# Hedgehog attention into a ReGLU feed-forward: first keys turned in fp32 on TensorE, a new head of the order

## The chip, the cores and the metric

One core of one Trainium2 chip runs the whole program. The metric is device time in microseconds of one execution; of several executions the median counts. A profiled execution also has a span, from its first to its last instruction, which is a little shorter than its time. The engines are named as in the profile: PE (TensorE), DVE (VectorE), ACT (ScalarE), POOL (GpSimd), SP (SyncE, which here only issues transfers).

## The reference

Eight batches, eight heads, 576 tokens of 64 numbers, all in float32. `phi` projects a token by the 64x128 matrix `w_phi`, takes the largest absolute value away and keeps both exponentials. The output of the attention, one row of 512 numbers a token, goes through a feed-forward with a ReLU gate (512 to 1536 and back).

```python
def phi(x):
    proj = np.einsum('bhsd,df->bhsf', x, w_phi)
    proj = proj - np.max(np.abs(proj), axis=-1, keepdims=True)
    return np.concatenate([np.exp(proj), np.exp(-proj)], axis=-1)
kv = np.einsum('bhsf,bhsd->bhfd', k_p, v)
num = np.einsum('bhsf,bhfd->bhsd', q_p, kv)
den = np.einsum('bhsf,bhf->bhs', q_p, z)[..., None] + 1e-06
gate = np.maximum(x @ w_gate, 0.0)
return (gate * (x @ w_val) @ w_out)
```

## The kernel before

All engines are programmed by one list of words, `ORDER`. Each word is a step (`do_..`), its arguments, after a colon the PSUM banks it uses, after an at sign the slot of a ring of buffers that it takes. There is no scheduler: on every engine the instructions stand in the order of the words, and an engine that waits holds up all that stands behind it on that engine. Waits between engines come from the tiles that the steps read and write.

A batch b is worked on in 512 tokens (a token row p holds tokens 4p to 4p+3, called i = 0 to 3) and 64 left over, which go two batches at a time into a ninth, mixed tile. The eight heads are cut in three groups j: heads 0 and 1, 2 to 4, 5 to 7. The mixed tokens of the keys ride with group 0, as its third "head".

- Loads. `lf` (SP, line 445) brings keys of heads 2 to 4 of batch 0 as fp32 into a tile that is free at that time, `cf` and `cg` (DVE and ACT, line 453) cast them to bf16. `lk`, `lq`, `lm` load the other keys, the queries and the mixed keys through POOL, which casts them on the way (lines 434, 466, 473); `lv` and `lw` load v and its mixed tokens (496, 520); `wl` and `wo` load thirds of the three large weights through POOL (528, 534). `wr` loads `w_phi` from ACT's queue (393), `wd` casts it on DVE (402), `w1` and `wa` make a second arrangement of it on PE and ACT.
- Keys of batch 0. `k0` turns six blocks of 128x128 on PE (584), `k1` copies them to kT on DVE (587), `k2` projects a group with twelve matmuls into four banks, one for each i (605). `ke` on ACT takes the two exponentials of each bank into kp (614), `kx` on DVE its largest absolute values into mk (622). `kk` (ACT, 631) makes from mk the two factors ek by which v is scaled; `kp` (ACT, 642) writes the same factors into 24 spare columns of a bank, from where DVE can read them.
- v. `vs` scales a group of v on POOL by ek (669), `vd` does it on DVE with the factors in the bank (651), `vo` and `vp` fill the last column on POOL and DVE (681, 659), `vq` scales the mixed v (line 697, POOL). Before, in batch 0, groups 0 and 1 and the mixed v are POOL's, group 2 DVE's. `kv` is the product of kp and the scaled v on PE (718), copied by ACT (`kc`, 729).
- Queries. `q0`, `q1`, `qb` turn and project them (746, 754, 764; from batch 1 on `qt`, `qc`, 769 and 778), `qe` takes the exponentials on ACT (793), `qx` the largest absolute values on DVE into maxq (801), `qy` turns maxq on PE (811), `qz`, `qu`, `qw` make of it the factor cq for one i.
- Attention's output. `nu` multiplies by kv (841), `nt` and `nv` join the halves on DVE (862, 872), `nr` takes the reciprocal (880), `nx` scales on POOL into xu (884). In batch 0 `xp` on PE and `xa` on ACT turn xu into xT (906, 920); later batches go by a transposing transfer, `xt`.
- Feed-forward. `pv` and `pg` (1029) are the value and gate products of one i in batch 0, four blocks of f at a time, `fv` and `fg` (1000) those of a whole group of 512 tokens. `pa`, `va` copy to val on ACT, `pb`, `ga` multiply on DVE (1050, 1021); `fo` is the product with w_out (1061), `fp` the last ones in halves (1092).
- `zz.n` is n matmuls of zeros, 128x256, into a bank that nobody reads (425). They have no place in the result; they stand in the first 28 us.

Of the kernel before, what the change touches and what calls it, by code (L numbers as in the profile page):

```python
# [16 lines left out]
ms.0 ms.4@vr0 wr ms.3@vr1 lf id sl ms.5 ms.6 ms.2 lw.0.1 lw.0.0 if cf.1 lk.0.2 lk.0.0 wd cg.0  # L17
zz.18:0 k0.1:0 k1.1:0@kT0 lm.0.1 lm.0.0 zz.1:1 w1:2 lq.0.1 lq.0.0 wa:2 zz.2:1 k2.1:0345
ke.0.1.2.0:4@kp0 lv.0.2 kx.0.1.1:3@mk0 lv.0.1 ke.0.1.3.1:5 kx.0.1.2:4 zz.2:1 k0.2:2 k1.2:2@kT1
ke.0.1.1.0:3 ke.0.1.2.1:4 kx.0.1.0:0 kx.0.1.3:5 ke.0.1.1.1:3 zz.7:1 k2.2:2674 ke.0.2.0.1:2@kp1  # L20
ke.0.2.2.0:7 kx.0.2.1:6@mk1 ke.0.2.0.0:2 ke.0.1.0.0:0 k0.0:3 k1.0:3@kT1 wl.0.0 ke.0.1.3.0:5
kx.0.2.2:7 kx.0.2.0:2 lv.0.0 zz.6:1 q0.1:3 q1.1:3@qT0 ke.0.2.1.1:6 ke.0.2.2.1:7 kx.0.2.3:4 zz.1:1
q0.0:5 q1.0:5@qT1 ke.0.2.1.0:6 zz.4:1 k2.0:2736 lm.1.1 lk.1.3 lm.1.0 kx.0.0.0:2@mk2 ke.0.1.0.1:0
kx.0.0.2:3 ke.0.2.3.0:4 kx.0.0.1:7 kp.0.2.1:4 kk.0.1.0@ek0 lq.1.2 kk.0.1.1 qb.1.0:0 qe.0.1.0.1:0@qp0
vo.1@vs0 kp.0.2.0:4 kx.0.0.3:6 vp.2:4@vs1 vs.0.1.0 qb.1.1:5 qe.0.1.1.0:5@qp1 qe.0.1.0.0:0 qx.0.1.1:5
ke.0.0.1.0:7@kp2 qx.0.1.0:0 vd.0.2.0:4 vs.0.1.1 kk.0.0.0@ek1 ke.0.0.3.0:6 zz.18:1 qb.0.1:0
ke.0.0.2.1:3 ke.0.0.1.1:7 qx.0.0.1:0 qb.0.2:7 qx.0.0.2:7 ke.0.2.3.1:4 wl.0.1 kk.0.0.1 vq.0.1
ke.0.0.0.1:2 ke.0.0.3.1:6 ke.0.0.0.0:2 zz.6:1 qb.0.0:6 vs.0.0.0@vs2 vq.0.0 qx.0.0.0:6 zz.5:1
# [1124 lines left out]
```

## Time and profile before

| what | value |
|---|---|
| three timed runs | 376.44, 376.68, 373.83 us; median 376.44 |
| the profiled execution's own time | 377.31 us |
| its span | 375.5 us |
| PE busy, share of the span | 367.3 us, 98% |
| DVE busy | 290.4 us, 77% |
| ACT busy | 228.5 us, 61% |
| POOL busy | 157.3 us, 42% |
| mean granted TensorE clock | 0.990 |

The profiled execution takes 1.8 us more than its span and is 0.87 us above the median of the runs. A timeline row holds start, duration, engine, line, operation, output and input, and a count where neighbours were merged; in square brackets stands how long the engine was idle before it and what ended that. The view by windows gives for each stretch its length and then, for each engine, busy time and number of instructions, the granted clock, the share of the DMA engines and what they moved.

### The profile page before, as it was taken

Reading aid. Unit: us, or ns where it says so; the run is one execution under the profiler, and the core shown is the slowest. Engines: PE = TensorE matmul, PEld = TensorE weight load, DVE = VectorE, ACT = ScalarE, POOL = GpSimd, SP = SyncE. Lnnn points to the kernel's source line nnn. Section 1 sums busy time; section 2 is a strip of 40 time slices with the busy share of each in tenths; the row PEclk is TensorE's granted clock in tenths of the full one; section 3 lists DMA queues with packets and bytes.
Section 4 is the critical chain, followed back from the end, with each engine's and each line's share of the span. In section 5 each row is a group of like instructions: output and inputs, shape, how many; then the busy total and the mean of one; then the engine's idle time right before and its main releaser. Section 6 shows DMA issues by size and latency. Waiting matters only on the chain.

```text
span 375.5 us, 9202 instructions
## 1 busy us (share of the span) xinstructions
PE 367.3 (98%) x3614; PEld 196.7 (52%) x3614; DVE 290.4 (77%) x672; ACT 228.5 (61%) x550; POOL 157.3 (42%) x163
## 2 busy tenths in 40 slices
PE   8798999999999999999999999999999999999996
PEld 5567857446544554564455444554444644444444
DVE  5969999998989899999978795888675646534441
ACT  4979996999768873987865556846764301212111
POOL 8774496549349138912770343513045013100000
PEclk9969999999999999999999999999999999999999
DMA  9999998973974992393438052183330022200114
GB/s 141 248 201 199 149 133 119 151 117 58 176 184 71 181 139 70 68 190 76 100 61 152 17 95 66 46 148 51 107 89 17 2 72 82 58 2 15 41 30 141
DMA packets 90381, 38.10 MB, mean 101 GB/s; under 512 B 64226, under 2 KB 85602, under 8 KB 90338
## 3 DMA queue, kind: packets, MB, share of 16 engines
q0 software_dynamic: 33504, 15.03, 31.4%
q1 hardware_dynamic: 56560, 22.29, 26.7%
q8 instruction: 28, 0.46, 0.5%
q10 hardware_dynamic: 274, 0.20, 0.2%
q14 instruction: 15, 0.12, 0.1%
HBM read 37.81 MB, written 9.44 MB: 126 GB/s over the span
## 4 chain that ended last, share of the span: by engine, by line
PE 93%; DVE 2%; DMA 2%; POOL 1%; ACT 1%; issue 0%; POOLq 0%; ACTq 0%
PE bank L1000 47%; PE bank L1061 24%; PE bank L718 6%; PE bank L841 4%; PE bank L1029 4%; PE bank L778 2%; PE bank L562 2%; DMA qn<-in_q_dram 2%; PE bank L982 1%; PE bank L1092 1%; PE bank L764 0%; PE bank L425 0%; POOL kn L434 0%; DVE mk L622 0%; DVE u L872 0%
## 5 line engine op out<-in xcount | busy, mean ns | idle before, releaser
L1061 PE MATMUL bank<-wo,h 128*128 128x512 bf16 x420 | 97.8, 379 | 0.0
L614 ACT ACTIVATE kp<-bank 128x384 bf16<-128x384 f32 x192 | 83.5, 509 | 16.4 <-PE bank L562 11.2
L1015 ACT CAST val<-bank 128x512 bf16<-128x512 f32 x81 | 47.2, 594 | 73.1 <-PE bank L1000 67.5
L1021 DVE SCALAR_TENSOR_TENSOR h<-bank,val 128x512 bf16<-128x512 f32 x100 | 67.1, 681 | 28.9 <-PE bank L1000 14.4
L1000 PE MATMUL bank<-xTs,wv 128*128 128x512 bf16 x352 | 87.1, 379 | 0.0
L1000 PE MATMUL bank<-xTs,wg 128*128 128x512 bf16 x352 | 86.4, 379 | 0.0
L884 POOL TENSOR_TENSOR xu<-u,r 128x512 bf16<-128x512 f32 x36 | 37.2, 1040 | 99.2 <-DVE r L880 72.5
L793 ACT ACTIVATE qp<-bank 128x512 bf16<-128x512 f32 x128 | 70.0, 619 | 10.7 <-PE bank L778 9.0
L1061 PEld LDWEIGHTS <-h 128*128 128x128 bf16 x420 | 39.2, 98 | 45.8 <-issue 2.4
L669 POOL TENSOR_TENSOR vs<-vn,ek 128x780 bf16<-128x780 f32 (+3 forms) x40 | 52.8, 1341 | 24.0 <-ACT ek L631 13.4
L1000 PEld LDWEIGHTS <-wg 128*128 128x128 bf16 x400 | 37.5, 98 | 41.6 <-issue 1.1
L1000 PEld LDWEIGHTS <-wv 128*128 128x128 bf16 x400 | 37.0, 98 | 41.1 <-issue 1.3
L622 DVE TENSOR_REDUCE mk<-bank 128x3 f32<-128x384 f32 x96 | 49.7, 541 | 3.5 <-ACT kp L614 1.4
L801 DVE TRANSPOSE_TENSOR_REDUCE maxq<-bank 128x16 f32<-128x512 f32 x64 | 42.4, 693 | 7.1 <-ACT qp L793 3.2
L872 DVE TENSOR_TENSOR u<-bank,t 128x195 f32<-128x195 f32 (+1 forms) x108 | 33.8, 331 | 2.4 <-POOL xu L884 0.4
L862 DVE TENSOR_TENSOR t<-bank,cq 128x195 f32<-128x195 f32 (+1 forms) x96 | 29.9, 327 | 7.0 <-PE bank L841 6.2
L841 PEld LDWEIGHTS <-qp 128*128 128x128 bf16 x512 | 22.5, 98 | 11.9 <-issue 1.5
L697 POOL TENSOR_TENSOR vr<-vm,ek 64x520 bf16<-64x520 f32 x16 | 16.9, 1055 | 23.4 <-ACT ek L631 15.9
L841 PE MATMUL bank<-kv,qp 128*128 128x65 bf16 x512 | 25.3, 193 | 0.0
L718 PEld LDWEIGHTS <-kp 128*128 128x128 bf16 x640 | 23.0, 101 | 3.9 <-ACT qp L793 1.0
L718 PE MATMUL bank<-vs,kp 128*128 128x65 bf16 x512 | 23.8, 198 | 0.0
L1070 ACT COPY ob<-bank 128x512 f32<-128x512 f32 x19 | 11.3, 595 | 20.4 <-PE bank L1061 19.5
(97 smaller groups left out, 355.2 us busy)
## 6 DMA issues: line engine op xcount, KB each, us to landing
out_dram<-ob SPq DMA_DIRECT2D x31, 256.0 KB, 2.4
vn<-in_v_dram SPq DMA_DIRECT2D x24, 256.0 KB, 4.2
kn<-in_k_dram POOLq DMA_DIRECT2D x7, 512.0 KB, 9.7
qn<-in_q_dram POOLq DMA_DIRECT2D x7, 512.0 KB, 7.6
wv<-in_moe_w_val_dram POOLq DMA_DIRECT2D x3, 512.0 KB, 11.4
wg<-in_moe_w_gate_dram POOLq DMA_DIRECT2D x3, 512.0 KB, 8.6
wo<-in_moe_w_out_dram POOLq DMA_DIRECT2D x3, 512.0 KB, 7.7
out_dram<-ob SPq DMA_DIRECT2D x9, 128.0 KB, 2.3
```

Of the source, the lines that this page charges most:

```text
L614: nc.scalar.activation(kp_of(3 * b + j)[:, i, s].rearrange("p n f -> p (n f)"), bank[bk[0]][:, 0 : 3 * F], AF.Exp, scale=(1.0, -1.0)[s],)
L622: nc.vector.tensor_reduce(mk_of(3 * b + j)[:, :, i], bank[bk[0]][:, 0 : 3 * F].rearrange("p (n f) -> p n f", f=F), axis=AX.X, op=ALU.max, ...
L669: nc.gpsimd.tensor_tensor(vs_of(3 * b + j)[:, s, 0:n].rearrange("p n i e -> p (n i) e")[:, :, 0:e], src[:, lo:hi].rearrange("p h i e -> p ...
L718: nc.tensor.matmul(out_ps[:, h - lo, s, :], lhsT=lhsT, rhs=rhs, start=(at == 0), stop=(at == 2 * n * (C + 1) - 1),)
L793: nc.scalar.activation(qp_of(4 * b + i)[:, s, 4 * hq : 4 * hq + 4].rearrange("p h m -> p (h m)"), bank[bk[0]], AF.Exp, scale=(1.0, -1.0)[s],)
L801: nc.vector.tensor_reduce(maxq[:, :, i, 4 * hq : 4 * hq + 4].rearrange("p t h -> p h t"), bank[bk[0]].rearrange("p (h t u) -> p h t u", h= ...
L841: nc.tensor.matmul(bank[bk[0]][:, E * n : E * (n + 1)], lhsT=qp_of(4 * b + i)[:, s, h, :], rhs=kv_of(b)[:, h, s, 0:E],)
L884: eng.tensor_tensor(xu_of(n).rearrange("p (h d) -> p h d", d=D), u_of(n)[:, :, 0:D], r_of(n).to_broadcast([P, H, D]), op=ALU.mult,)
L1000: nc.tensor.matmul(bank[bk[0]], lhsT=w[:, dc, P * f : P * f + P], rhs=xT(g)[:, dc, :], start=(dc == 0), stop=(dc == NDC - 1),)
L1015: nc.scalar.copy(val_of(NFC * g + f), bank[bk[0]])
L1021: nc.vector.scalar_tensor_tensor(h2_of(g, f), bank[bk[0]], 0.0, val_of(NFC * g + f), op0=ALU.max, op1=ALU.mult)
L1061: nc.tensor.matmul(bank[bk[0]], lhsT=h2_of(g, f)[:, P * t : P * t + P], rhs=wo_sb[:, f, :], start=(f == 0), stop=(f == NFC - 1),)
```

## The change

The words of `ORDER` are all new from the first one on, but not the work: apart from the start of batch 0, before and after hold the same steps. From `qc.2.1` on, which starts at 81.7 us in the profile of before, PE's 418 steps are the same in the same sequence. What differs by step:

- `kf`, `kh`, `kg`, `k3` for the first group (heads 2 to 4) in place of `cf`, `cg`, `k0.1`, `k1.1`, `k2.1`: PE turns the fp32 keys as they came, six blocks of 128x128 fp32 in two banks, ACT copies the one half (pairs i = 0, 1) and DVE the other to kT as bf16, and `k3` projects half a group (two values of i) with six matmuls into two banks. The other groups are projected by `k3` halves too, in place of `k2`.
- `wq` in place of `wr`: `w_phi` is loaded from SP's queue, behind `lf`.
- Batch 0's v: DVE now scales group 0 (`vd`, eight blocks of 64 in place of twelve) and the mixed v (`vz`, new, two instructions), with factors from bank 2; POOL scales group 2 in place of group 0 and the mixed v.
- Batch 0's query maxima go to four separate tables, one for each i (`maxq0`, in a part of h2 that is not yet used), so that `qy` for one i reads only that table. It is set to zero by `ms.9`.
- `zz`: 76 zero matmuls instead of 75, 20 times instead of 12, in smaller groups.
- Rings: mk and ek have 6 buffers, vs 4, qp 5 (before 3, 3, 3, 4). `nh` and `ni` are defined and not used.

```diff
-    mk_of = ring("mk", 3, [P, 3, 4], FP32)
-    ek_of = ring("ek", 3, [P, 2, 3, 4], FP32)
-    vs_of = ring("vs", 3, [P, 2, 3, 4, EP], BF16)
+    mk_of = ring("mk", 6, [P, 3, 4], FP32)
+    ek_of = ring("ek", 6, [P, 2, 3, 4], FP32)
+    vs_of = ring("vs", 4, [P, 2, 3, 4, EP], BF16)
...
-ms.0 ms.4@vr0 wr ms.3@vr1 lf id sl ms.5 ms.6 ms.2 lw.0.1 lw.0.0 if cf.1 lk.0.2 lk.0.0 wd cg.0
+ms.0 lf ms.2 lm.0.0 ms.4@vr0 ms.6 id lk.0.2 lk.0.0 wq ms.3@vr1 if ms.5 zz.12:7 kf.0:0 ms.9 kf.1:1 wd
...
+    def do_kf(bk, cp):
+        for n in range(3):
+            nc.tensor.matmul(
+                bank[bk[0]][:, P * n : P * n + P],
+                lhsT=k_first()[:, n, P * cp : P * cp + P],
+                rhs=identf,
+                is_transpose=True,
+            )
...
+    def do_k3(bk, j, cp):
+        T = kT_of(j).rearrange("p n m a -> p (n m a)").rearrange("p (k m) -> p k m", m=P)
+        heads = [1, 2, 0] if j == 0 else [0, 1, 2]
+        for k_, n in enumerate(heads):
+            for e in range(2):
+                r = slice(D * e, D * (e + 1))
+                nc.tensor.matmul(
+                    bank[bk[e]][:, F * n : F * (n + 1)],
+                    lhsT=T[r, 2 * k_ + cp, :],
+                    rhs=w64[r, :],
+                    start=(k_ == 0),
+                    stop=(k_ == 2),
+                )
+
+    def do_vz(bk, hh):
+        r = slice(SM * hh, SM * (hh + 1))
+        nc.vector.tensor_tensor(
+            vr_of(0)[r, :, :, hh, 0:E],
+            vm_of(0)[r][:, None, :, :].to_broadcast([SM, 2, 4, E]),
+            bank[bk[0]][r, 3 * F : 3 * F + 24]
+            .rearrange("p (s n i) -> p s n i", s=2, n=3)[:, :, 0, :, None]
+            .to_broadcast([SM, 2, 4, E]),
+            op=ALU.mult,
+        )
...
     def do_qx(bk, b, hq, i):
         nc.vector.tensor_reduce(
-            maxq[:, :, i, 4 * hq : 4 * hq + 4].rearrange("p t h -> p h t"),
+            (maxq0[:, i] if b == 0 else maxq)[:, :, i, 4 * hq : 4 * hq + 4].rearrange("p t h -> p h t"),
```

On DVE, from the cast of the first keys on, the order of before is this (kn are the keys in bf16, w64 is `w_phi`, mk the maxima of a group, qT the turned queries):

```order
L453 COPY kn_0_71<-xTm_144 128x256
L402 COPY w64_148<-w64f_146 128x128
L587 COPY kT_0_77<-bank0_63 128x768
L622 TENSOR_REDUCE mk_0_85<-bank3_66 128x3
L622 TENSOR_REDUCE mk_0_85<-bank4_67 128x3
L587 COPY kT_1_78<-bank2_65 128x768
```

and in the changed kernel, at the same place:

```order
L404 COPY w64_156<-w64f_154 128x128
L376 COPY sel_158<-ident_157 64x256
L627 COPY kT_0_77<-bank1_64 128x3x128
L669 TENSOR_REDUCE mk_0_85<-bank3_66 128x3
L669 TENSOR_REDUCE mk_0_85<-bank2_65 128x3
L669 TENSOR_REDUCE mk_0_85<-bank5_68 128x3
L590 COPY kT_1_78<-bank0_63 128x768
```

The cast is gone, the copy to kT is half as long and stands behind the cast of `w_phi`, and three of the four maxima of the first group now stand ahead of the second group's copy.

On POOL, from the start of batch 0's scaled v on, before (vs is the scaled v, vr the scaled mixed v, xu the attention's output, wv and wg the weights of the value and gate products, qm mixed queries):

```order
L681 COPY vs_0_91<-ek_0_88 128x24
L669 TENSOR_TENSOR vs_0_91<-vn_0_75,ek_0_88 128x12x64 x2
L528 DMA wv_141<-in_moe_w_val_dram 128x4x512
L697 TENSOR_TENSOR vr_1_95<-vm_0_76,ek_1_89 64x8x65
...
L681 COPY vs_2_93<-ek_1_89 128x2x8
L528 DMA wg_140<-in_moe_w_gate_dram 128x4x512 x2
L528 DMA wv_141<-in_moe_w_val_dram 128x4x512
L484 DMA qm_0_74<-in_q_dram 64x8x64
L884 TENSOR_TENSOR xu_0_124<-u_0_118,r_0_121 128x512
```

and after:

```order
L730 COPY vs_2_99<-ek_1_92 128x24
L718 TENSOR_TENSOR vs_2_99<-vn_0_75,ek_1_92 128x12x64 x2
L481 DMA km_0_72<-in_k_dram 128x1x128
L531 DMA wg_148<-in_moe_w_gate_dram 128x4x512
...
L933 TENSOR_TENSOR xu_2_134<-u_2_128,r_2_131 128x512
L481 DMA km_0_72<-in_k_dram 128x1x128
L933 TENSOR_TENSOR xu_3_135<-u_0_126,r_0_129 128x512
L531 DMA wv_149<-in_moe_w_val_dram 128x4x512
L730 COPY vs_3_100<-ek_2_93 128x24
L531 DMA wg_148<-in_moe_w_gate_dram 128x4x512
```

The scaled mixed v is gone from POOL; the last third of wv, which was issued ahead of the first xu, now stands behind all four of them, and the last third of wg behind a copy of batch 1's factors.

513 lines of the change are left out of this document (268 added, 245 removed).

## Prediction

> **What bounds the kernel now.** I read the page first, then the view by windows, cut where the clock or the kind of work changes, then the timeline of the first 46 us. The page:
>
> ```profile
> PE 367.3 (98%) x3614; PEld 196.7 (52%) x3614; DVE 290.4 (77%) x672; ACT 228.5 (61%) x550; POOL 157.3 (42%) x163
> PEclk9969999999999999999999999999999999999999
> PE 93%; DVE 2%; DMA 2%; POOL 1%; ACT 1%; issue 0%; POOLq 0%; ACTq 0%
> ```
>
> The span is PE's: 93% of the chain that ended last is matmuls. One slice, the third, has a clock of 0.6. The windows tell where time can be won (length, then busy time and count of PE, PEld, DVE, ACT, POOL; granted clock, DMA, GB/s):
>
> ```profile
> 7.00:16.40 9.40, 7.94 (x96) 5.67 (x93) 9.02 (x19) 8.97 (x26) 7.55 (x10) 1.00 1.26 243
> 16.40:19.80 3.40, 2.03 (x12) 0.97 (x12) 2.72 (x5) 2.77 (x10) 2.65 (x4) 1.00 1.47 188
> 19.80:23.20 3.40, 3.39 (x16) 1.02 (x15) 2.91 (x5) 3.40 (x8) 3.40 (x5) 0.51 1.37 202
> 23.20:26.70 3.50, 3.50 (x62) 3.44 (x60) 1.96 (x5) 1.41 (x4) 2.57 (x4) 0.50 1.17 207
> 26.70:32.10 5.40, 4.30 (x102) 3.48 (x101) 5.04 (x23) 5.19 (x15) 1.07 (x2) 1.00 1.22 197
> 32.10:37.50 5.40, 5.38 (x97) 4.67 (x97) 5.27 (x18) 5.30 (x13) 2.80 (x3) 1.00 1.30 198
> 37.50:46.10 8.60, 8.60 (x167) 7.82 (x165) 8.60 (x17) 7.78 (x20) 3.91 (x5) 1.00 1.14 161
> 46.10:81.70 35.60, 35.58 (x458) 20.27 (x458) 34.55 (x86) 31.53 (x83) 21.93 (x24) 1.00 1.08 138
> 81.70:375.50 293.80, 290.63 (x2590) 145.39 (x2589) 217.07 (x491) 159.85 (x378) 105.17 (x97) 1.00 0.44 83
> ```
>
> From 32.1 us on PE has no hole but the last 3 us, where the last rows leave; behind 81.7 its order is untouched. So the change can only move the point at which PE becomes full, and whether DVE, busy 34.55 of 35.60 us up to 81.7, lets PE stay full. Three things are seen ahead of 32.1: DVE and ACT are nearly full from 7 us on, PE waits for them between 16.4 and 19.8 (2.03 of 3.40), and after that PE runs 6.9 us at half clock, just when batch 0's kv is made.
>
> **First keys.** The rows of today, from the landing of the fp32 keys to the first exponential:
>
> ```profile
> 1.06 4.02 PE L425 MATMUL bank<-zero 128*128 128x256 bf16 x18 [1.06 <-DVE zero L412]
> 4.05 0.43 DVE L453 CAST kn<-xTm 128x256 bf16<-128x256 f32 x1 [0.91 <-DMA xTm<-in_k_dram]
> 4.87 0.85 PE L584 MATMUL bank<-ident,kn 128*128 128x128 bf16 x6
> 5.64 0.28 DVE L402 CAST w<-w64f 128x128 bf16<-128x128 f32 x1 [1.16 <-DMA w64f<-in_w_phi_dram]
> 5.79 0.55 DVE L587 COPY kT<-bank 128x768 bf16<-128x768 bf16 x1
> 6.59 0.51 PE L605 MATMUL bank<-w,kT 64*128 64x128 bf16 x12
> 7.13 6.08 ACT L614 ACTIVATE kp<-bank 128x384 bf16<-128x384 f32 x15 [0.39 <-PE bank L605]
> 7.40 0.34 PEld L584 LDWEIGHTS <-kn 128*128 128x128 bf16 x6 [0.26 <-DMA kn<-in_k_dram]
> 26.18 0.64 PE L811 MATMUL bank<-identf,maxq 128*128 128x128 f32 x2
> 26.41 0.49 ACT L729 CAST kv<-bank 128x390 bf16<-128x390 f32 x1 [0.67 <-PE bank L718]
> ```
>
> Keys land at 4.05 and the first exponential starts at 7.13. In the changed kernel the cast is gone. Twelve zeros end near 1.06 + 12 x 0.22 = 3.7, so PE stands free. An fp32 transpose is shown by L811: two take 0.64 at half clock, so three take about 0.85: 4.95. ACT's copy of half a group is nearest to L729, 0.49: 5.5. Six projections in place of twelve, half of 0.51 plus the pipe: 6.0. The first exponential starts at 6.05, 1.1 us earlier; DVE's half copy ends near 6.2, and its first maximum stands 0.8 us earlier than today. fp32 transposes are bounded by 0.6 (full clock) and 1.3 (twice the row), which moves this by 0.25 less or 0.45 more.
>
> This needs `w_phi` by 5.5. Today its cast waits until 5.64 and would end at 5.92; if the new queue brings nothing, the first exponential comes at 6.5, 0.6 us earlier than today and not 1.1. On SP's queue it is issued second, ahead of both loads of mixed v that now fill the queue, so I take the early end. [...] POOL's first transfer is now the half of the mixed keys, so the keys of the next group are issued one such issue later; I let PE have them at 7.5, where it takes them off the transfer at 7.40 today.
>
> **From there to the first kv.** Rows for the prices on DVE, and for what PE waits for:
>
> ```profile
> 12.12 0.62 PE L746 MATMUL bank<-ident,qn 128*128 128x128 bf16 x8 [0.57 <-DMA qn<-in_q_dram]
> 13.60 1.95 DVE L622 TENSOR_REDUCE mk<-bank 128x3 f32<-128x384 f32 x4
> 16.78 0.92 DVE L651 TENSOR_TENSOR vs<-vn,bank 128x768 bf16<-128x768 f32 x1
> 17.62 1.30 DVE L801 TRANSPOSE_TENSOR_REDUCE maxq<-bank 128x16 f32<-128x512 f32 x2
> 18.53 1.05 POOL L697 TENSOR_TENSOR vr<-vm,ek 64x520 bf16<-64x520 f32 x1 [0.67 <-issue]
> 22.89 0.40 PE L718 MATMUL bank<-vs,kp 128*128 128x65 bf16 x4
> 23.16 0.41 PE L718 MATMUL bank<-vs,kp 128*128 128x65 bf16 x4
> 26.82 0.29 PE L718 MATMUL bank<-vs,kp 128*128 128x65 bf16 x4
> 26.97 0.29 PE L718 MATMUL bank<-vs,kp 128*128 128x65 bf16 x4
> 27.24 0.19 PE L718 MATMUL bank<-vr,kp 128*128 128x65 bf16 x1
> 26.93 0.29 DVE L819 TENSOR_REDUCE my<-bank 128x32 f32<-128x128 f32 x1 [1.77 <-ACT kv L729]
> 29.85 1.04 POOL L884 TENSOR_TENSOR xu<-u,r 128x512 bf16<-128x512 f32 x1 [4.08 <-DVE r L880]
> 32.10 1.05 PE L1029 MATMUL bank<-xTs,wv 128*128 128x128 bf16 x16
> 37.46 1.06 PE L1029 MATMUL bank<-xTs,wg 128*128 128x128 bf16 x16
> ```
>
> The first kv now belongs to group 0, whose v DVE scales. DVE has to do ahead of it: twelve maxima of keys at 0.47 (1.95 for four, overlapping) = 5.6; three copies to kT at 0.5 (0.55 with its end overlapping), 1.5; two of queries, a third longer, 1.2; four query maxima at 0.6 = 2.4; two `vd`. These have 512 numbers where 768 take 0.85 from start to start (16.78 to 17.62), so 0.6 each, 1.2. Two `vz`, which nobody shows: 520 numbers a row. The bounds are 0.5 (520 over 768 of the 0.85, less some start) and 1.05 (the same product on POOL, 18.53); I take 0.65, since DVE's own row is the nearer, 1.3 in all. Small reductions and transposes and the last column: 0.8, at 0.29 and less for one (26.93). Sum 14.0, from 5.75: 19.8. Waits that stay, for the second keys (7.5), the third, and `qy`: about 1.2. The first kv starts at 21.0 in place of 22.89. POOL is not late: it loses 2.1 us of mixed v and takes twelve blocks in place of eight. The queries' landing (12.12) does not move, and it delays the second half of the keys' projections, not the first.
>
> Then the clock. Five kv matmuls start every 0.27 us at half clock (22.89, 23.16) and every 0.15 at full (26.82, 26.97). Today kv and two `qy` last until 27.4. In the changed kernel the holes at 16.4 to 19.8 are filled: 17 zeros and the two `qy` stand there among the `qb`, and I take the clock as full. Sixteen times 0.15 is 2.4: kv ends at 23.5, the last copy near 23.9. DVE comes to the first t and u at about 23.7, after three more maxima and a transpose; the new split of maxq removes the 1.77 us that it waits at 26.93. From 26.93 to xu at 29.85 DVE needs 2.9 us today for the small reductions, the t and u of one i and their reciprocal; about as much again from 23.7 lets xu start at 26.6, 3.2 us earlier. From xu to the first value product today takes 2.25 us; ACT's order adds 0.25: 29.1 for 32.10. At 37.46 PE has done four such products and the queries of batch 1; the same set takes 5.4 us again: 34.5. PE's own gain is 3.0 us.
>
> **What DVE lets stand.** DVE is busy 70.1 us between 7.0 and 81.7 (its windows added up). The change adds 1.3 (`vz`), takes 0.5 (`vd`), and two instructions of 0.9 together stand behind `qc.2.1` now. Its first maximum comes 0.8 us earlier, so with today's 4.6 us of idle time it would gain only 0.8 or so. By my walk its idle time up to 37 us falls from 3.6 to 1.7: a gain of 2.7. If all idle went, 5. I take 2.8 for the whole, between PE's 3.0 and DVE's 2.7. Everything behind 81.7 us keeps its order and its distance. So 377.31 - 2.8 = 374.5 for the profiled execution; that one stood 0.87 above the median, so 376.44 - 2.8 = 373.6 us.
>
> **Rivals.**
>
> 1. DVE does not fill its holes: it gains 0.8 and PE is held to that, 375.6. For it speaks that DVE and ACT were all but full from 26.7 to 46.1 us; against it that PE's waits today have other owners (the copy of kv, xu).
>
> 2. The clock falls again. Today it fell after the stretch with 2.03 busy of 3.40, and came back only after 3.50 of 3.50. If the zeros are too few, kv costs 16 x 0.12 = 1.9 us more: 375.5. [...]
>
> 3. The last third of the value weights is late, and the kernel is slower. It was issued before the first xu; now it stands behind all four (37.82 today, some 37.0 then), and 4-matmul value products that need it start at 46.10 today, 43.3 with all gains, 45 or so by the new order.
>
> ```profile
> L528 POOL DMA_DIRECT2D wv<-in_moe_w_val_dram x3: 751/760/813, 7.6 to 24.3; - x3
> DMA to landing us min/median/max: 9.2/11.4/13.6
> 46.10 1.90 PE L1000 MATMUL bank<-xTs,wv 128*128 128x512 bf16 x8
> 37.82 1.04 POOL L884 TENSOR_TENSOR xu<-u,r 128x512 bf16<-128x512 f32 x1 [1.28 <-DVE r L880]
> ```
>
> 37.0 + 9.2 = 46.2, 1 us late; with the median, 48.4, 3 us late, which is where it decides: a landing over 10.8 us eats the gain. With 13.6 PE stands for 5.6 us: 373.6 + 5.6 = 379.2, and a fallen clock on top passes 380. Against it: the loads of v for batch 1, which shared the DMA engines in those 13.6 us, are then through.
>
> 4. DVE and ACT run without holes and PE follows: DVE gains 5, 371.4.
>
> **How the numbers follow.** The forecast, a gain of 1.8 to 4.3 (372.1 to 374.6), has 0.52; rival 1 0.12, rival 2 0.12, rival 3 0.12, rival 4 0.12. The predicted time is the forecast's, 373.6. For 8 in 10 the range leaves out half of rival 3 and a part of rival 4: 371.2 to 377.2. A measurement of this kernel tells about 1% from no change, 3.8 us. Faster than 372.7: rival 4 and a third of the forecast, 0.30. Slower than 380.2: the end of rival 3, with the clock, 0.08. Within 1%: 0.62.
>
> **What would show it.** Right: the first exponential at 6.0 to 6.5, the first kv at 20.5 to 21.5 with five matmuls every 0.15, xu at 26 to 27, the first value product before 29.5, `qc.2.1` at 78.5 to 79.5, and from there a trace that only lies earlier. Wrong: a clock of 0.5 anywhere behind 7 us, DVE holes of over 2 us between 7 and 37, PE idle for wv ahead of the first 4-matmul products, or PE less than full between 32 and 80.

## The result, and the profile after

The median of nine executions is 371.84 us (371.79 to 373.32), beside 374.63 us for the kernel before (nine executions, 373.82 to 376.68): a ratio of 0.9926, 95% interval 0.9904 to 0.9948, so 0.5 to 1.0% less. The forecast was 373.6 us, a gain of 2.8 us, no difference over 1%. The difference of the medians is 2.79 us, but the time itself lies 1.8 us below the forecast, just outside the 372.1 to 374.6 us that the prediction gave to it, and inside its wide range. The forecast took its gain off the 376.44 us of its three executions, and nine have a lower median; the two profiled executions lie 5.5 us apart (377.31 and 371.81 us). So 2.79 beside 2.8 is no proof of the sum, and its parts have to be looked at one by one. One execution of the experiment h1 below, at 468.72 us with a granted clock of 0.755, counts in its median and is left out of its range.

From the page of the changed kernel: PE's row, the granted clock by slices, and the engines' shares of the chain that ended last.

```profile
PE 363.5 (98%) x3615; PEld 195.2 (53%) x3615; DVE 289.0 (78%) x674; ACT 227.1 (61%) x550; POOL 156.5 (42%) x161
PEclk9999999999999999999999999999999999999999
PE 94%; DVE 2%; DMA 1%; ACT 1%; issue 0%; SPq 0%; ACTq 0%
```

The slice with 0.6 is gone, and PE is busy 3.8 us less with the same products and one zero matmul more. The view by windows, with the cuts of the prediction (length, then busy time and count of PE, PEld, DVE, ACT, POOL; granted clock, DMA, GB/s):

```profile
7.00:16.40 9.40, 9.26 (x100) 6.19 (x100) 9.36 (x19) 9.36 (x30) 7.29 (x9) 1.00 1.28 250
16.40:19.80 3.40, 3.38 (x20) 1.42 (x19) 3.23 (x10) 3.40 (x9) 3.39 (x4) 1.00 1.45 199
19.80:23.20 3.40, 3.40 (x97) 3.27 (x95) 3.34 (x6) 3.37 (x9) 3.40 (x5) 1.00 1.31 202
23.20:26.70 3.50, 3.24 (x60) 2.34 (x59) 3.50 (x16) 3.31 (x9) 1.05 (x2) 1.00 1.24 206
26.70:32.10 5.40, 5.16 (x103) 5.04 (x104) 5.40 (x22) 5.18 (x14) 2.10 (x3) 1.00 1.25 198
32.10:37.50 5.40, 5.40 (x97) 4.85 (x94) 5.35 (x12) 5.36 (x14) 3.96 (x6) 1.00 0.91 169
37.50:46.10 8.60, 8.60 (x157) 7.38 (x155) 8.55 (x15) 8.33 (x22) 8.51 (x10) 1.00 1.40 188
46.10:81.70 35.60, 35.60 (x422) 18.52 (x420) 34.69 (x89) 31.29 (x83) 24.49 (x26) 1.00 1.02 140
81.70:370.00 288.30, 285.12 (x2553) 143.41 (x2551) 212.24 (x482) 155.40 (x369) 96.44 (x90) 1.00 0.44 84
```

DVE's third column, added up from 7.0 to 37.5 us, is 30.18 of 30.50 us: 0.3 us of idle time, where the kernel before had 3.6 and the prediction left 1.7. The clock is 1.00 throughout, and PE never waits for the last third of the value weights (8.60 of 8.60). The timeline at the places that the prediction named (start, length, work, count, and the idle time ahead of it with its releaser):

```profile
4.31 0.89 PE L618 MATMUL bank<-identf,xTm 128*128 128x128 f32 x6 [0.52 <-DMA xTm<-in_k_dram]
5.92 0.33 DVE L404 CAST w<-w64f 128x128 bf16<-128x128 f32 x1 [2.37 <-DMA w64f<-in_w_phi_dram]
6.30 0.34 PE L641 MATMUL bank<-w,kT 64*128 64x128 bf16 x6 [1.10 <-DVE w L404]
6.67 0.49 ACT L661 ACTIVATE kp<-bank 128x384 bf16<-128x384 f32 x1 [1.27 <-PE bank L641]
7.61 0.50 PE L587 MATMUL bank<-ident,kn 128*128 128x128 bf16 x6
20.21 0.29 PE L767 MATMUL bank<-vs,kp 128*128 128x65 bf16 x4
20.36 0.29 PE L767 MATMUL bank<-vs,kp 128*128 128x65 bf16 x4
22.32 1.01 ACT L778 CAST kv<-bank 128x390 bf16<-128x390 f32 x2
25.68 1.03 POOL L933 TENSOR_TENSOR xu<-u,r 128x512 bf16<-128x512 f32 x1 [2.45 <-DVE r L929]
27.88 1.05 PE L1093 MATMUL bank<-xTs,wv 128*128 128x128 bf16 x16 [0.24 <-ACT xTs L984]
77.17 0.40 PE L827 MATMUL bank<-qT,w 32*128 32x512 bf16 x4
```

The first exponential comes at 6.67, 0.46 us earlier than before, and not at 6.05: PE stands 1.10 us for w_phi. The first kv starts at 20.21, five matmuls every 0.15 us; xu at 25.68, the first value product at 27.88, and `qc.2.1` (the row at 77.17) is 4.5 us earlier than in the profiled execution before. Of the landmarks that the prediction named, the first exponential comes later than its range; the first kv, xu and `qc.2.1` come earlier than theirs, and the first value product lies within. None of its signs of being wrong is seen.

### The profile page after: what moved, and what is told of

It reads as the page before. It is cut to its first block, busy times and chain, and to the rows that moved or that the text cites. A ratio compares the mean times of both kernels' runs of the same rounds, so it can differ in the third digit from the quotient of the medians.

```text
span 370.0 us, 9211 instructions
## 1 busy us (share of the span) xinstructions
PE 363.5 (98%) x3615; PEld 195.2 (53%) x3615; DVE 289.0 (78%) x674; ACT 227.1 (61%) x550; POOL 156.5 (42%) x161
## 4 chain that ended last, share of the span: by engine, by line
PE 94%; DVE 2%; DMA 1%; ACT 1%; issue 0%; SPq 0%; ACTq 0%
PE bank L1064 47%; PE bank L1125 25%; PE bank L767 5%; PE bank L890 4%; PE bank L1093 4%; PE bank L565 3%; PE bank L827 2%; DMA w64f<-in_w_phi_dram 1%; PE bank L428 1%; ACT kp L661 1%; DVE h L850 1%; PE bank L1046 1%; PE bank L1156 1%; DVE vr L651 0%; PE bank L813 0%; PE bank L860 0%
## 5 line engine op out<-in xcount | busy, mean ns | idle before, releaser
L842 ACT ACTIVATE qp<-bank 128x512 bf16<-128x512 f32 x128 | 69.2, 620 | 10.7 <-PE bank L827 9.4
L718 POOL TENSOR_TENSOR vs<-vn,ek 128x780 bf16<-128x780 f32 (+2 forms) x40 | 53.7, 1363 | 23.8 <-ACT ek L678 13.3
L850 DVE TRANSPOSE_TENSOR_REDUCE maxq<-bank 128x16 f32<-128x512 f32 x56 | 37.4, 691 | 6.2 <-ACT qp L842 3.3
L890 PEld LDWEIGHTS <-qp 128*128 128x128 bf16 x512 | 23.1, 98 | 12.6 <-issue 2.0
L890 PE MATMUL bank<-kv,qp 128*128 128x65 bf16 x512 | 26.1, 193 | 0.3 <-ACT kv L778 0.2
L1137 DVE COPY ob<-bank 128x512 f32<-128x512 f32 x16 | 10.9, 683 | 16.1 <-PE bank L1125 13.8
L746 POOL TENSOR_TENSOR vr<-vm,ek 64x520 bf16<-64x520 f32 x14 | 14.8, 1057 | 20.2 <-ACT ek L678 10.1
L767 PEld LDWEIGHTS <-kp 128*128 128x128 bf16 x640 | 21.6, 97 | 2.8 <-ACT qp L842 0.2
(104 smaller groups left out, 371.8 us busy)
```

The lines of the kernel that those rows point to most:

```text
L718: nc.gpsimd.tensor_tensor(vs_of(3 * b + j)[:, s, 0:n].rearrange("p n i e -> p (n i) e")[:, :, 0:e], src[:, lo:hi].rearrange("p h i e -> p ...
L767: nc.tensor.matmul(out_ps[:, h - lo, s, :], lhsT=lhsT, rhs=rhs, start=(at == 0), stop=(at == 2 * n * (C + 1) - 1),)
L842: nc.scalar.activation(qp_of(4 * b + i)[:, s, 4 * hq : 4 * hq + 4].rearrange("p h m -> p (h m)"), bank[bk[0]], AF.Exp, scale=(1.0, -1.0)[s],)
L850: nc.vector.tensor_reduce((maxq0[:, i] if b == 0 else maxq)[:, :, i, 4 * hq : 4 * hq + 4].rearrange("p t h -> p h t"), bank[bk[0]].rearran ...
L890: nc.tensor.matmul(bank[bk[0]][:, E * n : E * (n + 1)], lhsT=qp_of(4 * b + i)[:, s, h, :], rhs=kv_of(b)[:, h, s, 0:E],)
```

## The experiments

Twelve kernels ran beside the kernel before. Step names are those of the order; a step's start is that of its record in the trace. Four landmarks of each profiled execution turned out to be enough. They are the first exponential, `q1.0` (the copy of the second half of the queries), the start of kv's last copy, and the start of ScalarE's last copy of the output (`o1.7.2`).

| kernel | first exp. | q1.0 | last kv copy | last copy out | between these two | median, range of all executions |
|---|---|---|---|---|---|---|
| before, profiled | 7.13 | 12.85 | 27.47 | 372.46 | 344.99 | 374.63, 373.82 to 376.68 |
| changed | 6.67 | 12.94 | 22.84 | 366.90 | 344.06 | 371.84, 371.79 to 373.32 |
| b0 before again | 7.24 | 12.55 | 24.43 | 369.73 | 345.30 | 374.20, 373.84 to 377.46 |
| e1 before, more zeros | 7.38 | 12.70 | 24.62 | 369.33 | 344.71 | 374.25, 373.84 to 375.86 |
| e2 fewer zeros at kv | 6.67 | 13.76 | 24.94 | 369.00 | 344.06 | 373.54, 373.03 to 374.18 |
| e3 first keys cast | 7.12 | 15.47 | 25.51 | 369.65 | 344.14 | 374.77, 373.88 to 376.24 |
| f1 clock early | 6.68 | 13.04 | 23.15 | 367.20 | 344.05 | 372.05, 371.87 to 372.43 |
| f2 clock late | 6.83 | 14.85 | 24.89 | 368.93 | 344.04 | 373.68, 373.09 to 374.09 |
| f3 cast, clock early | 7.28 | 13.69 | 23.69 | 367.94 | 344.25 | 372.78, 372.26 to 373.57 |
| f4 old tail | 6.86 | 14.23 | 24.17 | 370.47 | 346.30 | 375.34, 374.03 to 376.09 |
| g1 w_phi first | 8.04 | 15.27 | 25.12 | 369.16 | 344.04 | 374.31, 373.83 to 376.40 |
| g3 mixed v on GpSimd | 6.67 | 13.02 | 24.89 | 368.90 | 344.01 | 374.89, 373.62 to 376.07 |
| g4 one maxq | 6.68 | 14.15 | 24.79 | 368.83 | 344.04 | 373.64, 372.40 to 373.91 |
| h1 w_phi alone | 6.67 | 12.94 | 22.91 | 366.97 | 344.06 | 372.62, 372.26 to 373.53 |

The sixth column is the main finding. In all ten kernels with the changed tail (all but the two traces of the kernel before, e1 and f4), kv's last copy and the last copy of the output stand 344.0 to 344.3 us apart, while the copy itself moves by 2.7 us. What happens ahead of that copy is found at the end one for one, and nothing behind it makes up for it. The other four take 344.7 to 346.3 us.

### The clock of the kernel before: b0 and e1

b0 is the kernel before without an edit.

> The kernel before, unchanged, to see several executions with their granted clock. Theory A: its half clock from 19.84 to 26.67 us comes only in some executions, because the stretch ahead of it (16.4 to 19.8 us, 2.03 us of PE work in 3.40) stands on the edge. Then the executions split by their granted clock: about 0.99 with 376.0 to 377.3 us, about 1.0 with 373.8 to 374.8 us. Rival: the clock falls in every execution, and the spread of 3 us comes from elsewhere; then the granted clock is 0.99 in all of them, whatever the time.

The executions split: eight at 373.84 to 374.55 us with a granted clock of 0.998 to 1.0, four at 376.46 to 377.46 with 0.989 to 0.990. Of the 96 other executions of the kernel before that ran beside the experiments, 34 have 0.995 or less (375.96 to 377.74, median 376.92) and 62 have 0.999 or 1.0 (373.81 to 375.83, median 374.50). Theory A holds. b0's profiled execution is one without the fall; its windows, and its timeline at kv, at `qc.2.1` and at the first kv of batch 2:

```profile
16.40:19.80 3.40, 2.53 (x14) 1.10 (x13) 2.72 (x5) 2.96 (x10) 2.87 (x4) 1.00 1.48 189
19.80:23.20 3.40, 3.20 (x65) 2.24 (x66) 3.40 (x7) 3.40 (x9) 3.40 (x6) 1.00 1.39 201
23.20:26.70 3.50, 3.33 (x87) 2.73 (x83) 3.40 (x16) 3.50 (x11) 2.11 (x3) 1.00 1.25 228
```

```profile
21.42 0.30 PE L718 MATMUL bank<-vs,kp 128*128 128x65 bf16 x4
21.58 0.29 PE L718 MATMUL bank<-vs,kp 128*128 128x65 bf16 x4
78.62 0.63 PE L778 MATMUL bank<-qT,w 32*128 32x512 bf16 x8
86.74 0.28 PE L718 MATMUL bank<-vs,kp 128*128 128x65 bf16 x4 [0.37 <-POOL vs L669]
```

The same program makes five kv matmuls every 0.16 us here, and 0.27 in the profile that the prediction was made from. Its kv ends 3.0 us earlier (24.43 for 27.47) and `qc.2.1` starts 3.06 us earlier than at 81.68. So the half clock at kv was an event of that execution, as of a third of all, and worth 3 us; the fair profile to hold the change against is b0's: a gain of 1.45 us at `qc.2.1`, 2.8 us in the span (372.8 for 370.0).

e1 puts 15 zeros more into two gaps of the kernel before:

```diff
-zz.18:1 qb.0.1:0
+zz.26:1 qb.0.1:0
-zz.6:1 qb.0.0:6
+zz.13:1 qb.0.0:6
```

> The kernel before with 15 more zero matmuls in two gaps of PE (8 ahead of qb.0.1 at 16.04 to 16.92 us, 7 ahead of qb.0.0 at 18.35 to 19.20 us), nothing else. Theory A (the fallen clock at kv costs time in the executions that have it): no clock of 0.5 behind 6 us, kv's matmuls five per 0.15 us, qc.2.1 1 to 2 us earlier than the 81.7 us of the profiled execution before, the median 373.5 to 374.5 us and the spread under 1.5 us. Rival B (DVE sets the pace in the head, the clock is covered): qc.2.1 within 0.5 us of 81.7 and the median as that of the kernel before.

```profile
16.40:19.80 3.40, 3.38 (x25) 1.85 (x22) 2.66 (x5) 2.96 (x9) 2.87 (x4) 1.00 1.48 186
```

PE is busy 3.38 of 3.40 us in that stretch, none of the 12 executions has a clock of 0.995 or less, and the highest is 375.86 us. `qc.2.1` comes at 78.75, 2.9 us earlier (more than expected), and the median is 374.25 (ratio 0.9985, 0.9967 to 1.0003), in the expected range; the spread is 2.0 us, not under 1.5. The median hardly moves because two thirds of the executions of the kernel before have no fall; what is gone is the slower third. That the half clock at kv is on the path is shown. Zeros alone do not reach the changed kernel: 2.4 us are left.

### The zeros at kv in the changed kernel: e2

```diff
-qb.1.1:5 zz.3:7 qb.0.1:4
+qb.1.1:5 qb.0.1:4
...
-vs.0.2.1 zz.7:7 kv.0.0:6
+vs.0.2.1 kv.0.0:6
```

The edit takes out 30 of the 76 zero matmuls, where the expectation says 32.

> The changed kernel without the 32 zero matmuls between 13.5 and 20.4 us, nothing else. Theory A (the zeros keep the clock, and the clock at kv is on the path): a clock of 0.5 for about 6.8 us that takes in kv, kv's matmuls five per 0.27 us, the last copy of kv 1.5 to 2 us later than 23.34, and the time 1.3 to 2.5 us above the changed kernel. Rival B (the clock is covered by DVE): same clock, but qc.2.1 less than 0.7 us later than 77.2. Rival C (PE's own work keeps the clock without zeros): no 0.5, times as the changed kernel.

```profile
16.40:19.80 3.40, 2.34 (x6) 0.60 (x7) 3.40 (x10) 3.40 (x10) 3.40 (x5) 0.77 1.43 195
19.80:23.20 3.40, 3.06 (x54) 2.98 (x54) 3.31 (x7) 3.24 (x8) 3.40 (x5) 0.50 1.32 201
23.20:26.70 3.50, 3.43 (x62) 3.04 (x60) 2.18 (x6) 2.25 (x6) 0.65 (x1) 0.73 1.26 200
```

The clock falls (0.77, 0.50, 0.73), in the trace from 18.23 to 25.05 us, and to 0.991 to 0.995 in all 12 executions. The last copy of kv comes 2.1 us later, and so does the end; the median is 1.7 us above the changed kernel's. Theory A: the time is as expected, kv 0.1 us above its range. The third row shows how it costs: DVE is busy 2.18 of 3.50 us, and all of the rest is one wait for the first product that reads kv (L890 is `nu`; the view of waits gives the total, the number and the longest):

```profile
DVE t L911 <- PE bank L890: 1.3, 1, 1.3
```

### First keys, and the clock before 12 us: e3, f2, f3, f1

e3 casts the first keys and turns them in bf16, as before:

```diff
-zz.12:7 kf.0:0 ms.9 kf.1:1 wd kh.0:0@kT0 sl k3.1.0:23
+ms.9 cf.1 cg.0 zz.12:7 wd k0.1:0 k1.1:0@kT0 sl k3.1.0:23
-w1:4 kg.1:1
+w1:4
```

> The changed kernel with the first keys as in the kernel before: cast by DVE and ACT, six bf16 transposes, one copy of 768 by DVE, in place of six fp32 transposes and two half copies; the projections, the new order and w_phi's queue stay. Theory A (DVE is full from its first maximum on, so what the first keys win stays to the end): the first exponential 0.3 to 0.6 us later than 6.67, qc.2.1 later by as much, the time 0.3 to 0.6 us more. Prediction's own term: 0.8 to 1.1 us more. Rival B (slack behind takes it): the first exponential later, qc.2.1 and the time within 0.15 us of the changed kernel.

All three missed. The first exponential is 0.45 us later, as expected, but the queries' copy 2.5 us, kv 2.7 us and the median 2.9 us (ratio to the kernel before 0.9989, 0.9968 to 1.0010). A reason is seen in PE's timeline: the six transposes of the next keys, 0.50 us in the changed kernel (the row at 7.61), take 0.85.

```profile
9.03 0.85 PE L587 MATMUL bank<-ident,kn 128*128 128x128 bf16 x6
```

Its first full clock is recorded at 12.15 us, the changed kernel's at 4.43. A new theory: the time of the first grant matters by itself. f2 takes 10 of the first 12 zeros away and leaves the first keys as changed:

```diff
-zz.12:7 kf.0:0
+zz.2:7 kf.0:0
```

> The changed kernel with 2 in place of 12 zero matmuls ahead of the first transposes, nothing else. Theory A: the full clock is granted at 9 us or later, the twelve maxima of keys come later by 0.5 to 1.5 us because PE makes transposes and projections at half clock, and the time is 372.8 to 374.5 us. Rival B (DVE and ACT cover PE's half clock in the first 12 us): a late grant, but kv.0.0 within 0.3 us of 20.21 and the time 371.8 us.

```profile
4.21 1.52 PE L618 MATMUL bank<-identf,xTm 128*128 128x128 f32 x6 [2.54 <-DMA xTm<-in_k_dram]
8.53 0.85 PE L587 MATMUL bank<-ident,kn 128*128 128x128 bf16 x6
9.41 0.56 DVE L590 COPY kT<-bank 128x768 bf16<-128x768 bf16 x1 [0.84 <-PE bank L587]
```

The grant comes at 11.41 us, DVE waits 0.84 us for the transposes, the last of the twelve maxima starts at 15.91 in place of 14.00 (0.4 us more than expected), kv is 2.05 us later, and the median 1.84 us. Theory A is shown: a PE at half clock in the first 12 us is on the path through DVE. f3 gives e3 its clock back with more zeros:

```diff
-zz.12:7 wd k0.1:0 k1.1:0@kT0 sl k3.1.0:23
+zz.17:7 wd k0.1:0 k1.1:0@kT0 sl zz.4:7 k3.1.0:23
```

> The changed kernel with the first keys cast and turned in bf16, as in the experiment with cast first keys, but with 9 more zero matmuls (17 in place of 12 at the start, 4 ahead of the first projection) so that the clock comes up. Theory A (of the 2.9 us that the cast first keys cost, all but the later first exponential is the clock, granted at 12.15 us there): the full clock by 8 us, the first exponential at 7.0 to 7.2, qc.2.1 0.4 to 0.7 us later than 77.17, the time 372.2 to 372.6 us. Rival B (the form of the first keys itself costs it): the time stays at 374.0 us or more with the clock up.

Granted at 6.90 us; the first exponential at 7.28, `qc.2.1` and kv 0.85 us later than in the changed kernel, the median 0.94 us above. That is theory A with 0.1 to 0.2 us more than its ranges, and rival B is out. So of e3's 2.9 us some 2 were the clock, and the fp32 form of the first keys is worth 0.9 us or somewhat less: the grant still came 2.5 us later than in the changed kernel's profile. f1 adds 7 zeros to the changed kernel:

```diff
-zz.12:7 kf.0:0 ms.9 kf.1:1 wd kh.0:0@kT0 sl k3.1.0:23
+zz.14:7 kf.0:0 ms.9 kf.1:1 wd kh.0:0@kT0 sl zz.5:7 k3.1.0:23
```

> The changed kernel with 7 more zero matmuls in PE's first gaps (14 in place of 12 ahead of the fp32 transposes, 5 between them and the first projection, where PE waits for w_phi), nothing else. [...]

Its profile has the first full clock at 4.18 us. Six executions lie at 371.87 to 372.43 us (371.7 to 372.3 was the range set for all of them), against 371.79 to 373.32 in nine of the changed kernel: the group at 373.2 is not among them, though six are few, and the first grant is known for the profiled one alone. The median is not lower (372.05; ratio to the kernel before beside it 0.9902, 0.9871 to 0.9933). Two other kernels with the changed first 9 us show what the group at 373.2 is likely to be: f4's profile has its first grant at 9.68 us and `q1.0` at 14.23, g4's has the full clock from 3.78 to 7.20, half until 10.61, and `q1.0` at 14.15; both are 1.2 to 1.3 us late at that point. No trace of an execution of the group itself was taken.

### VectorE's part and the table of maxima: g3, g4

g3 gives mixed v back to GpSimd:

```diff
-kp.0.0.0:2 ke.0.2.0.0:3
+kp.0.0.0:2 kk.0.0.0@ek2 ke.0.2.0.0:3
-kp.0.0.1:2 kk.0.2.0
+kp.0.0.1:2 kk.0.0.1 kk.0.2.0
-vs.0.1.1 qe.0.1.1.1:5
+vs.0.1.1 vq.0.0 vq.0.1 qe.0.1.1.1:5
-wl.0.0 vz.0:2 qb.0.2:4
+wl.0.0 qb.0.2:4
-qu.0.0@mz1 vz.1:2
+qu.0.0@mz1
```

> The changed kernel with mixed v of batch 0 scaled by GpSimd, as in the kernel before (two multiplications of 520 numbers a row, ahead of the second head group's, and two exponentials by ScalarE for them) in place of VectorE's two; heads 0 and 1 stay with VectorE. Theory A (GpSimd becomes the last releaser of kv): the last group's v is ready about 1.5 to 2.1 us later, the last copy of kv 0.7 to 1.5 us later than 22.84, the time 0.5 to 1.5 us more. Rival B (VectorE sets the pace and is relieved of 1.4 us): kv at most 0.3 us later, the time 0 to 1 us less.

```profile
16.75 2.20 POOL L746 TENSOR_TENSOR vr<-vm,ek 64x520 bf16<-64x520 f32 x2
19.91 2.91 POOL L718 TENSOR_TENSOR vs<-vn,ek 128x768 bf16<-128x768 f32 x2
22.87 0.28 PE L767 MATMUL bank<-vs,kp 128*128 128x65 bf16 x4 [1.50 <-ACT qp L842]
```

The releaser in PE's row is put down to ScalarE, but kv's second group starts 0.05 us after the second of GpSimd's two products (2.91 us together) ends at 22.82. kv's last copy is 2.05 us later, and the median 3.05 us higher. Theory A, above the expected size by 0.5 us at kv. Some 0.8 us of the median are something else: the profiled execution (374.09 us) is 2.28 us above the changed kernel's, and eight of the twelve lie at 374.81 us or more, four of these with a granted clock of 0.995; a stretch of half clock is likely, but no trace shows one of them. VectorE, relieved of 1.4 us, gains nothing.

g4 has one table of query maxima for batch 0:

```diff
-(maxq0[:, i] if b == 0 else maxq)
+maxq
```

> The changed kernel with one table for the query maxima of batch 0, as in the kernel before, in the new order. Theory A (each maximum of a next tile waits until PE has turned the table for the tile before, which is the 1.77 us that VectorE waited before): VectorE waits 0.2 to 0.7 us in all at the maxima between 16 and 26 us, the last copy of kv and the time later by that, 0.2 to 0.7 us. Rival B (the new order leaves room enough between turning and the next maximum): no wait over 0.1 us, the time within 0.15 us of the changed kernel.

```profile
17.88 0.72 DVE L850 TRANSPOSE_TENSOR_REDUCE maxq<-bank 128x16 f32<-128x512 f32 x1 [0.84 <-PE bank L860]
```

One wait of 0.84 us, a little above the expected range. Of the 1.95 us by which kv is late, 1.21 are there at `q1.0` already (the clock, above), and 0.74 are the table. Three of the seven executions lie at 372.40 to 372.66 us, 0.6 to 0.8 above the changed kernel's 371.8: theory A. But the 1.77 us that the expectation names are not what one table costs in the kernel before. b0 and e1 have the one table too, and VectorE's only wait there between 14 and 30 us is another one, for a projection of queries (from the view of waits, the same line in both: total, number, longest):

```profile
DVE maxq L801 <- PE bank L764: 0.7, 1, 0.7
```

Of the three traces only the profile before, where kv runs at half clock, has the 1.77 us.

### w_phi: g1, h1

g1 issues w_phi ahead of the first keys:

```diff
-ms.0 lf ms.2
+ms.0 wq lf ms.2
...
-lk.0.0 wq ms.3@vr1
+lk.0.0 ms.3@vr1
```

> The changed kernel with w_phi issued on SyncE's queue ahead of the first keys instead of behind them, nothing else. Theory A (PE's first projections wait 1.1 us for w_phi, whose packets share the time from 3.70 to 5.37 us with those of mixed v on the same queue): w_phi's cast before 4.5 us in place of 5.92, the keys at most 0.3 us later, the first exponential at 6.1 to 6.3 in place of 6.67, the last copy of kv 0.3 to 0.6 us earlier than 22.84, the time 371.2 to 371.6 us. Rival B (the keys lose what w_phi wins): the first exponential within 0.15 us of 6.67 and the time as that of the changed kernel. Rival C (the grant of the clock moves with the zeros' place in the head, and hides it): the executions spread over 1.5 us with other shares.

```profile
4.80 0.23 DVE L404 CAST w<-w64f 128x128 bf16<-128x128 f32 x1 [1.24 <-DMA w64f<-in_w_phi_dram]
6.06 1.51 PE L618 MATMUL bank<-identf,xTm 128*128 128x128 f32 x6 [2.27 <-DMA xTm<-in_k_dram]
```

w_phi's cast is 1.1 us earlier, but the transposes of the keys start at 6.06 in place of 4.31: not 0.3 us later but 1.75. In the trace the keys' packets run from 2.62 to 5.59 us, in the changed kernel from 1.85 to 3.76. None of the three expectations had that size; it is rival B's direction and far more. The end is 2.3 us later, the median 374.31. But this is not the price of the keys' delay alone: PE stands for 2.27 us ahead of the transposes, they run at half clock (1.51 us), and the first full clock comes at 10.16 us. In f2, f4 and g4 a half clock up to 11.41, 9.68 and 10.61 us went with 1.2 to 2.1 us at kv. Rival C had named this, and the executions spread over 2.6 us. No run separates the two.

h1 keeps the order and holds mixed v back:

```diff
-zz.12:7 kf.0:0 ms.9 kf.1:1 wd kh.0:0@kT0 sl k3.1.0:23
+zz.14:7 kf.0:0 ms.9 kf.1:1 wd kh.0:0@kT0 sl zz.3:7 k3.1.0:23
...
-lw.0.1 lq.0.0
+gt.1 lw.0.1 lq.0.0
```

> The changed kernel with a small copy (64 numbers of the first turned keys, to a tile nobody reads) on SyncE's queue ahead of the two loads of mixed v, so that these start only when the first keys are turned (6.8 us; they are needed at 18.4), and with 5 more zero matmuls in PE's first gaps (14 for 12 ahead of the fp32 transposes, 3 ahead of the first projection). Theory A (w_phi is late because its packets share the queue with mixed v's): its cast at 5.0 to 5.5 us in place of 5.92, the first exponential at 6.1 to 6.4, VectorE full from there on, the time 371.4 to 371.7 us in nearly all executions. Rival B (the loads on GpSimd's queue hold w_phi as much): cast and first exponential within 0.15 us of 5.92 and 6.67, the time as with the zeros alone, 371.9 to 372.2 us. Rival C (the first exponential comes earlier, but the queries' landing at 11 to 12 us holds VectorE): first exponential at 6.1 to 6.4 and the time 371.9 to 372.2 us.

```profile
5.77 0.48 DVE L404 CAST w<-w64f 128x128 bf16<-128x128 f32 x1 [2.21 <-DMA w64f<-in_w_phi_dram]
```

Rival B. With no mixed v on the queue, w_phi's packets still run from 3.62 to 5.33 us (3.70 to 5.37 in the changed kernel), and the first exponential stays at 6.67. The median is 372.62 us, 0.4 above B's range. So mixed v is not what holds w_phi. The loads on GpSimd's queue run in the same 2 us; whether they hold it was not tried.

### Behind qc.2.1: f4

In the changed order 1022 of the 1175 steps with a bank behind `qc.2.1` have another bank number, many buffers have other numbers, and some of the steps on VectorE, GpSimd and the queues have changed places, though PE's order is the same. f4 joins the changed head to the tail of the kernel before.

```diff
-qc.2.1:3215 ga.1.4:0@hs13 mn.0.1:7 qe.2.1.2.1:1 fg.1.6:4 ku.3
+ga.1.4:0@hs8 ku.3 qc.2.1:0126 qx.2.1.1:1 qe.2.1.2.1:2 qe.2.1.3.1:6
...
```

> The changed kernel up to qc.2.1, and behind it the order, the banks and the buffer numbers of the kernel before (numbers exchanged in pairs so that what lives across fits). The work is the same. PE's order behind qc.2.1 is that of both. Theory A (1022 of the 1175 bank numbers behind qc.2.1 are new in the change, and the new ones make PE wait less for banks; that is the 0.8 us that builds up between 85 and 310 us): qc.2.1 at 77.2, the last product's start 0.6 to 0.9 us later than 357.99, the time 372.4 to 372.8 us. Rival B (the tail runs better only because POOL and DVE come to it earlier): the time 371.8 to 372.0 us.

```profile
79.54 0.63 PE L834 MATMUL bank<-qT,w 32*128 32x512 bf16 x8 [0.99 <-DVE h L1092]
```

The median is 375.34 us, 3.5 above the changed kernel's. Its clock came late (1.33 us at kv); 1.0 us is the wait in the row, `qc.2.1` for a bank at the seam, which neither parent has; and from the exponential behind `qc.2.1` (`qe.2.1.2.1`) to `o1.7.2` it takes 290.23 us, where nine of the ten kernels with the changed tail take 289.0 to 289.1 (f3 289.2) and the three runs of the tail before 289.9 to 290.4.

Theory A is half right: `qc.2.1` at 79.54 and the median miss its ranges; the distance from there to the end goes its way, 1.2 us longer where 0.6 to 0.9 were expected, and 0.27 of that is one wait at 168 us for VectorE, which the other traces of the old tail do not have. Taken step by step, PE's work behind 85 us (of the changed kernel's time) falls back against the changed kernel by 0.85 us in all three traces of the tail before (from 4.70 to 5.56 us in the profile before, 1.58 to 2.43 in e1, 1.98 to 2.83 in b0), with no wait of PE in the records. What b0 has beyond that, 0.53 us, stands ahead of 85 us, most of it in its row at 86.74: 0.37 us for GpSimd's product, a wait that the changed kernel and e1 do not have.

```profile
168.40 0.28 PE L897 MATMUL bank<-kv,qp 128*128 128x65 bf16 x4 [0.27 <-DVE u L928]
84.76 0.29 PE L767 MATMUL bank<-vs,kp 128*128 128x65 bf16 x4
```

(The first row is f4's, the second the changed kernel's counterpart of b0's row.) So the new tail is worth 0.85 us and up to 0.5 more. Which of banks, buffers and changed places makes it was not taken apart.

No kernel tried has a lower median than the changed one; f1 has the smallest spread. What f3, g3 and g4 lose at kv (0.85, 2.05 and 0.74 us) is the price of taking one piece out of the new order; the three add up to more than the 1.6 us that the whole wins there against b0, and are not shares of it. `w_phi`'s old queue and the smaller rings were not tried by themselves in the new order.

## Why the prediction was right, point by point

Against b0 the gain is 2.83 us at `o1.7.2`: 1.59 at kv's last copy (24.43 to 22.84), -0.14 from there to `qe.2.1.2.1`, 1.38 behind it. The forecast had 2.8, all of it ahead of 81.7 us and none behind. That the number held is luck: two terms were off in opposite directions. Ahead of `qc.2.1` the gain against b0 is 1.45 us, half of what was forecast, because the sum takes away a fallen clock that most executions do not have; behind it a gain stands that the sum put at nothing.

- **First keys.** Predicted 1.1 us, or 0.6 if the new queue brought nothing for w_phi. It brought nothing: the cast starts at 5.92 (5.64 in the profile before, 5.87 in b0), and the first exponential gained 0.46. The step that failed is "so I take the early end": no run shows `w_phi` by 5.5 us behind the keys. Its cast starts at 5.92 in the changed kernel and at 5.77 in h1, and no first exponential of the table comes before 6.67. On ScalarE's queue too `w_phi`'s packets ran only when the keys' were nearly done (keys to 3.52 and `w_phi` 3.41 to 5.27 in the profile before, keys to 3.99 and 3.87 to 5.50 in b0). ScalarE's half copy ends at 5.39 for 5.5, but by two errors that cancel: the transposes start at 4.31 and not 4.05, and after 0.60 us three are there for the copy, where 0.85 was read off a row that ran mostly at half clock. In the changed kernel's trace the last packet of the keys starts at 3.71, the first of w_phi at 3.70: the weights follow right behind the keys. What no row had priced is that these 64 KB then take 1.7 us (to 5.37) beside the other loads.
- **First kv.** Predicted 21.0, measured 20.21. The sum of VectorE's work was right: 14.0 us predicted, and it is busy 13.9 us from 6.31 to the end of `vz.1` at 20.45. The waits were not: 1.2 us predicted, and it has 0.04 in the 9.4 us from 7 on and 0.17 in the next 3.4. `vz` takes 0.65 and 0.70 (0.65 taken), `vd` 0.65 and 0.67 (0.6). That this part of the change carries weight is shown by g3: with mixed v on GpSimd the kernel loses 2 us at kv.
- **The clock stays full.** It does in the profiled execution, and eight of the nine have a granted clock of 0.999 or 1.0; the ninth (373.32 us) has 0.995, and no trace tells where its half clock lay. e2 shows that the zeros do it. But 1.9 us was the price of kv's matmuls alone; b0 against the profiled execution shows 3.0 us at kv's last copy, 1.5 of them at the first kv already (22.89 for 21.42). And the term belongs to a third of the executions (38 of 108), not to all: this is a failed step too, the row of one execution taken for the kernel's. The prediction asked whether the clock falls and not how often. In the records the place of its changes differs from profile to profile: in g4 (3.78, 7.20 and 10.61 us) and in the profile before (6.19, 19.84 and 26.67) they lie multiples of 3.41 us apart, and over all profiles the first lies anywhere from 3.78 to 12.15 us.
- **The split of maxq.** Predicted to remove the 1.77 us of waiting at 26.93. This was a misreading of the row: there VectorE waits for the maxima that PE turns (L811 at 26.18), and these stand behind kv's matmuls at half clock. b0 and e1 have the one table and no fall, and do not have the wait (the row under g4). It is the clock a second time, another term of the sum that most executions do not have. In the new order one table costs 0.84 us of waiting and 0.74 at kv, so there the split is worth something.
- **PE's 3.0 and DVE's 2.7 us.** Rival 4 (no holes on DVE, 371.4 us) describes the profile better than the forecast, and its time is nearer: 0.3 us of idle time to 37.5 us, and 371.84. But b0, without the fallen clock, has 1.1 and not 3.6 (its DVE windows add up to 29.36 of 30.50), so most of that idle time was the clock's too. Rivals 1 and 2 did not come: DVE was full, and the clock held.
- **"Everything behind 81.7 us keeps its order and its distance".** Failed: PE's order is kept, its distance is not. The stretch behind `qe.2.1.2.1` is 1.05 us shorter than in the profile before and 1.4 shorter than in b0, and f4 takes 1.2 more with the old tail; 0.85 us is in all three traces of the old tail. The diff showed the new numbers; the prediction looked at the order of steps alone.
- **Rival 3.** The last third of the value weights did not make PE wait (35.60 of 35.60 us busy from 46.1). It was issued at 35.28 us and not 37.0, landed at 40.84, 5.6 us later where the prediction had 9.2 to 13.6, and was first used at 44.33.

## What to carry to other kernels

Before a sum is made against one profiled execution, ask which of its rows another execution of the same program need not have: a clock that fell in 38 of 108 executions is one (PE was busy 2.03 of the 3.40 us from 16.4 on in the profile with the fall, 2.53 in b0's without it), and the spread of the times shown (373.8 to 376.7 us) was the sign of it. Look for the one landmark behind which the distance to the end is constant; here it is kv's last copy (344.0 to 344.3 us in ten traces), and a single trace then prices an edit, provided that the clock's part is taken off first, which in g4 was 1.2 of 1.95 us. An order with the same steps on the bound engine can still take another time if its bank and buffer numbers, and the places of steps on the other engines, are new: here 0.85 us in all three traces of the old tail.

## What the runs showed of the hardware

- The first grant of the full clock came between 3.78 (g4) and 12.15 us (e3), for the same first instructions at 4.43 (the changed kernel), 9.68 (f4), or at 3.78 with a fall at 7.20 (g4); with half a clock until 11.41 us this kernel's last copy out is 2.03 us later and its median 1.84 us higher (f2).
- With 64 KB of weights in packets of 512 bytes issued ahead of the keys, the keys' transposes started 1.75 us later (6.06 for 4.31, g1); issued behind, the weights took 1.7 us themselves (3.70 to 5.37 us in the changed kernel; 3.62 to 5.33 with no mixed v on their queue, h1).
- Six fp32 transposes of 128x128 took 0.85 us at full clock (f1, g4; 0.89 in the changed kernel, with the grant just behind their start) and 1.51 to 1.52 at half (f2, f4, g1); six of bf16 took 0.50 to 0.51 at full (the changed kernel, f1, f3) and 0.82 to 0.85 at half (e3, f2, f4, g4).
